# Block-sparse attention and SwiGLU on one core: later rows transposed by DMA, zero-tile matmuls ahead of the mask, a finer split of the first batch

## Chip, cores, metric

One Trainium2 chip, one core. The metric is device microseconds of one execution. A profiled execution also has a span (first to last instruction); the time is 1.7 to 2.3 us longer than the span in these runs.

## The reference, cut to what matters

```python
# B, H, S, D = 4, 8, 768, 64; blocks of 32, three random blocks per block row
scores = scale * q @ k.T ; scores = where(mask, scores, -1e9)
attn   = softmax(scores) @ v                       # per batch and head
x  = attn.transpose(0, 2, 1, 3).reshape(3072, 512)
xn = x / sqrt(mean(x * x) + 1e-6) * rms_g          # the "normed rows"
out = (silu(xn @ w_gate) * (xn @ w_val)) @ w_out   # 512 -> 1536 -> 512
```

## The kernel before

Work is cut into units: a batch, a first tile of 128 tokens and a number of tiles. A unit goes through attention for four pairs of heads (`qk`, `exp`, `av`, `xo`), normalisation (`sq`, `rsq`, `xq`), a transpose of its rows (`tr` on PE, `cp` on ACT or DVE), and the three weight products (`g`, `v`, `y`). A list scheduler in the kernel, with a guessed duration for each operation, fixes the order of instructions on every engine before anything runs.

```python
UNITS = [(0, 0, 1), (0, 1, 2), (0, 3, 3)]
UNITS += [(b, c, 3) for b in range(1, B) for c in (0, 3)]
...
nc.scalar.dma_start(out=gB, in_=moe_rms_g.unsqueeze(0).to_broadcast([P, DM]))   # the RMS gain
...
def turn(g):                # K and Q of batches 1 to 3: 24 tiles of 128 x 128
    nc.sync.dma_start_transpose(out=X[g % NSLOT]..., in_=aug[g % NAUG]...)
...
def tr(u):                  # rows of a unit: 4 transposes per tile on PE
    for t in range(nt):
        for c in range(NP):
            nc.tensor.transpose(out=t_[:, t, c, :], in_=xqs[u][:, t, c * P:(c + 1) * P], identity=ident)

def cp(u, eng):             # PSUM -> SBUF
    xns[u] = work.tile([P, NP, nt * P], BF16, name="xn", tag="xn", bufs=NXN)
    ...
def proj(u, f, w_, kind, pool):
    ...
    nc.tensor.matmul(out=p_[:, j, :], lhsT=w_[:, c, f_ * P:(f_ + 1) * P],
                     rhs=xns[u][:, c, :], start=(c == 0), stop=(c == NP - 1))
...
FILL0 = {"DVE": 0.57, "POOL": 0.84}     # casts of the first batch: on DVE or GpSimd
op(("zp",), {"POOL": 1.8}, [], (9,), lambda e, p: zero_pad(), at=18.0)
```

The softmax here doesn't subtract the row's maximum and nothing guards it: scores larger than these inputs give would overflow.

## Time and profile before

| | before |
|---|---|
| time, median of the first 4 runs | 322.04 us (321.62 to 323.87) |
| span of the profiled execution | 321.1 us (its time: 323.15) |
| PE busy | 304.5 us, 95% |
| first gate matmul | 32.59 us |

Engines: PE is TensorE, PEld its weight loads, DVE VectorE, ACT ScalarE, POOL GpSimd, SP SyncE, which issues DMAs. A busy PE may still run at half rate, so what follows compares the spacing of matmuls and not only busy shares. The prediction shows the lines.

### The profile page before, as it was taken

The page shows a single profiled execution, that of the slowest core. Times are in us where ns is not written, and L with a number is a line of the kernel's source. Part 1 is how long each engine was busy: PE and PEld are TensorE (multiplying, and loading weights), DVE is VectorE, ACT ScalarE, POOL GpSimd, SP SyncE. Part 2 cuts the span into 40 slices and gives each one's busy share as a digit, 9 for nine tenths or more (in the row PEclk, how much of TensorE's full clock was granted, in tenths as well). Part 3 has the DMA queues.
Part 4 walks back from the last instruction along what each step waited for, and adds up shares of the span by engine and source line. Part 5 has one row for each costly group of instructions (what it writes and reads, how often), then busy time and mean ns, then how long its engine had stood idle before and what let it go on. Part 6 is the DMA issues. An engine that isn't in the chain of part 4 may idle for free.

```text
span 321.1 us, 7025 instructions
## 1 busy us (share of the span) xinstructions
PE 304.5 (95%) x2903; PEld 200.0 (62%) x2934; DVE 193.9 (60%) x416; ACT 210.3 (65%) x312; POOL 24.9 (8%) x41
## 2 busy tenths in 40 slices
PE   2997999997999999999999999999999999999995
PEld 2886887774567666666666666666655656545542
DVE  5595676695358769546754844584567737717600
ACT  3588878895689777877777877877725323333221
POOL 4493000100001001000000100010010000000000
PEclk9999999999899999999999999999999999999999
DMA  7999997989986999600765000000000000020022
GB/s 223 369 194 204 245 270 156 258 283 185 279 276 144 216 243 263 234 3 33 100 132 98 35 36 0 35 2 33 3 33 35 0 35 34 0 97 3 0 100 98
DMA packets 59779, 40.03 MB, mean 125 GB/s; under 512 B 38628, under 2 KB 56548, under 8 KB 59748
## 3 DMA queue, kind: packets, MB, share of 16 engines
q1 hardware_dynamic: 53776, 34.61, 39.9%
q0 software_dynamic: 5792, 4.72, 9.5%
q8 instruction: 23, 0.38, 0.5%
q10 hardware_dynamic: 180, 0.26, 0.2%
q14 instruction: 8, 0.07, 0.1%
HBM read 28.57 MB, written 6.29 MB: 109 GB/s over the span
## 4 chain that ended last, share of the span: by engine, by line
PE 89%; DVE 4%; DMA 3%; ACT 2%; issue 1%; ACTq 0%; DVEq 0%
PE gp L331 19%; PE vp L331 19%; PE yp L363 18%; DMA X<-aug 2%; PE tp L212 2%; ACT pt L246 2%; PE tr L306 2%; DVE aug L182 1%; DMA samp_i<-in_sampled_blocks_dram 1%; DVE xq L296 1%; DVE sc L282 1%; DVE hp L354 0%; DVE xo L272 0%; PE o__3874 L260 0%; PE o__1140 L260 0%
## 5 line engine op out<-in xcount | busy, mean ns | idle before, releaser
L345 DVE SCALAR_TENSOR_TENSOR uu<-th,gp 128x384 bf16<-128x384 bf16 (+1 forms) x93 | 52.5, 566 | 60.8 <-ACT th L339 59.0
L331 PE MATMUL vp<-xn,wv 128*128 128x384 bf16 (+2 forms) x432 | 75.1, 309 | 0.3 <-DVE hp L354 0.3
L331 PE MATMUL gp<-xn,wg 128*128 128x384 bf16 (+2 forms) x432 | 75.1, 309 | 0.0
L339 ACT ACTIVATE th<-gp 128x384 bf16<-128x384 f32 (+1 forms) x93 | 46.6, 503 | 32.6 <-PE gp L331 30.5
L363 PE MATMUL yp<-wo,hp 128*128 128x512 bf16 x257 | 66.1, 381 | 1.8 <-issue 0.2
L354 DVE TENSOR_TENSOR hp<-uu,vp 128x384 bf16<-128x384 bf16 (+1 forms) x93 | 50.9, 563 | 11.4 <-PE vp L331 10.5
L331 PEld LDWEIGHTS <-wg 128*128 128x128 bf16 x432 | 40.3, 98 | 24.3 <-issue 0.8
L235 PEld LDWEIGHTS <-X 88*128 88x128 bf16 x432 | 38.9, 100 | 26.4 <-issue 4.3
L331 PEld LDWEIGHTS <-wv 128*128 128x128 bf16 x432 | 40.2, 97 | 24.4 <-issue 0.5
L363 PEld LDWEIGHTS <-hp 128*128 128x128 bf16 x288 | 28.2, 98 | 28.3 <-issue 0.5
L260 PEld LDWEIGHTS <-pt 128*128 128x128 bf16 x1152 | 41.6, 98 | 5.1 <-ACT pt L246 0.3
L372 ACT ACTIVATE yo<-yp 128x512 f32<-128x512 f32 x18 | 10.8, 599 | 24.2 <-PE yp L363 24.0
L289 POOL TENSOR_TENSOR rs<-ms,nhalf 128x3 f32<-128x3 f32 (+2 forms) x9 | 7.3, 806 | 207.3 <-DVE ms L282 207.3
L182 DVE CAST aug<-qkv 128x768 bf16<-128x768 f32 x30 | 17.7, 602 | 5.4 <-DMA X<-aug 3.2
L296 DVE SCALAR_TENSOR_TENSOR xq<-xo,rs,gB 128x512 bf16<-128x512 f32 x24 | 16.7, 746 | 1.0 <-POOL rs L289 0.7
L282 DVE CUSTOM_DVE_ANT_0 sc<-xo 128x512 bf16<-128x512 f32 x24 | 16.6, 690 | 0.7
L314 ACT COPY xn<-tr 128x1536 bf16<-128x1536 bf16 x7 | 10.1, 1437 | 7.9 <-PE tr L306 7.9
L212 PE MATMUL tp<-ident,aug 128*88 128x128 bf16 x96 | 9.0, 257 | 1.6 <-DVE aug L182 1.2
L212 PEld LDWEIGHTS <-aug 128*88 128x88 bf16 x96 | 8.2, 149 | 2.4 <-DVE aug L182 1.5
L182 DVE COPY X<-tp 88x768 bf16<-88x768 bf16 (+2 forms) x17 | 7.5, 473 | 3.6 <-PE tp L212 3.4
L182 DVE CAST vaug<-qkv 128x768 bf16<-128x768 f32 x14 | 7.7, 552 | 0.9 <-DMA qkv<-in_v_dram 0.9
L306 PE MATMUL tr<-ident,xq 128*128 128x128 bf16 x96 | 7.0, 219 | 0.1
(529 smaller groups left out, 359.0 us busy)
## 6 DMA issues: line engine op xcount, KB each, us to landing
qkv<-in_k_dram SPq DMA_DIRECT2D x16, 384.0 KB, 6.1
qkv<-in_q_dram SPq DMA_DIRECT2D x16, 384.0 KB, 6.1
qkv<-in_v_dram SPq DMA_DIRECT2D x16, 384.0 KB, 8.0
out_dram<-yo SPq DMA_DIRECT2D x24, 256.0 KB, 2.8
wg<-in_moe_w_gate_dram POOLq DMA_DIRECT2D x4, 384.0 KB, 8.8
wv<-in_moe_w_val_dram POOLq DMA_DIRECT2D x4, 384.0 KB, 9.9
wo<-in_moe_w_out_dram POOLq DMA_DIRECT2D x2, 768.0 KB, 18.3
gB<-in_moe_rms_g_dram ACTq DMA_DIRECT2D x1, 256.0 KB
```

Of the source, the lines that this page charges most:

```text
L182: nc.vector.tensor_copy(out=out, in_=in_)
L212: nc.tensor.transpose(out=t_[0:KQ, m, :], in_=aug[g % NAUG][:, i, e, c, 0:KQ], identity=ident)
L235: nc.tensor.matmul(out=s_[:, e, j * w:(j + 1) * w], lhsT=x[0:KQ, 0, e, jt * P:(jt + 1) * P], rhs=x[0:KQ, 1, e, c0 * P:c0 * P + w], start=T ...
L260: nc.tensor.matmul(out=o_[:, t, e, :], lhsT=pt[:, jt, e, t * P:(t + 1) * P], rhs=va[:, (2 * pr + e) * NC + jt, 0:D + 1], start=(jt == 0), ...
L282: nc.vector.tensor_tensor_reduce(out=sc, in0=x, in1=x, scale=1.0 / DM, scalar=1e-6, op0=ALU.mult, op1=ALU.add, accum_out=mss[u][:, t:t + 1])
L296: nc.vector.scalar_tensor_tensor(out=xqs[u][:, t, :], in0=xos[u][:, t].rearrange("p h d -> p (h d)"), scalar=mss[u][:, t:t + 1], in1=gB, o ...
L306: nc.tensor.transpose(out=t_[:, t, c, :], in_=xqs[u][:, t, c * P:(c + 1) * P], identity=ident)
L331: nc.tensor.matmul(out=p_[:, j, :], lhsT=w_[:, c, f_ * P:(f_ + 1) * P], rhs=xns[u][:, c, :], start=(c == 0), stop=(c == NP - 1))
L339: nc.scalar.activation(out=t_, in_=tiles["gp", u, f], func=AF.Tanh, scale=0.5)
L345: nc.vector.scalar_tensor_tensor(out=t_, in0=tiles.pop(("th", u, f)), scalar=1.0, in1=tiles.pop(("gp", u, f)), op0=ALU.add, op1=ALU.mult)
L354: nc.vector.tensor_tensor(out=hps[u][:, f * fg:(f + 1) * fg, :], in0=tiles.pop(("uu", u, f)), in1=tiles.pop(("vp", u, f)), op=ALU.mult)
L363: nc.tensor.matmul(out=y_, lhsT=hps[u][:, f, t * P:(t + 1) * P], rhs=wo[:, f, :], start=(f == 0), stop=(f == NF - 1))
```

## The change

The intent is to take 72 PE transposes off the bound, to have PE at full rate when real work comes, and to bring the first unit's rows to the weight products earlier. The diff, cut to its core:

```diff
-    UNITS = [(0, 0, 1), (0, 1, 2), (0, 3, 3)]
+    UNITS = [(0, 0, 1), (0, 1, 1), (0, 2, 2), (0, 4, 2)]
...
+    zt = const.tile([P, 512], BF16, name="zt")
+    nc.vector.memset(zt, 0.0)
+    zp = ps_a.tile([P, 512], FP32, name="zp", tag="vp")
+    for i in range(NWARM):                                  # NWARM = 9
+        nc.tensor.matmul(out=zp, lhsT=zt[:, 0:P], rhs=zt, start=True, stop=True)
...
-    nc.scalar.dma_start(out=gB, ...)                        # early, ACT's queue
+    def load_g():                                           # SP, after the first four pairs
+        nc.sync.dma_start(out=gB, in_=moe_rms_g.unsqueeze(0).to_broadcast([P, DM]))
...
-        xns[u] = work.tile([P, NP, nt * P], BF16, name="xn", tag="xn", bufs=NXN)
+        xns[u] = work.tile([P, nt, NP, P], BF16, name="xn", tag="xn", bufs=NXN)
+    def xt(u):
+        nc.sync.dma_start_transpose(
+            out=xns[u].rearrange("p t c w -> p (t c) w"),
+            in_=xqs[u].rearrange("p t f -> p (t f)"))
-                    ... rhs=xns[u][:, c, :],
+                    ... rhs=xns[u][:, :, c, :],
...
-    op(("zp",), ..., at=18.0)
+    op(("zp",), ..., at=26.0)                               # zero fill, later
-        op(("wi", i), {"POOL": 2.2 if i < NWC else 1.2},
+        op(("wi", i), {"POOL": 1.8 if i < NWC else 1.0},    # weight issue, guessed shorter
+        if u < NPET:                                        # NPET = 4: tr and cp as before
+        else:
+            op(("cp", u), {"DMA": 1.8}, ..., lambda e, p, u=u: xt(u), ...)
...                                                         # guessed time to landing of turn: 2 -> 4 us
+        end[...] = fin + (8.0 if ... else 4.0 if o["key"][0] == "turn" else LAT[e])
```

The diff also lets the scheduler count the buffers of `th` and `uu`, and changes two more of its guesses (`sq` from 0.62 to 0.75 us, the start of the DMA queue from 1.8 to 2.1). No run takes these, or the later zero fill, alone.

More of the change, by code (lines that the diff above doesn't have):

```diff
@@ L44 @@
     KQ = D + NB
-    NSLOT, NAUG, NRAW = 5, 2, 3
-    UNITS = [(0, 0, 1), (0, 1, 2), (0, 3, 3)]
+    NSLOT, NAUG, NRAW, NWARM = 5, 2, 3, 9
+    UNITS = [(0, 0, 1), (0, 1, 1), (0, 2, 2), (0, 4, 2)]
     UNITS += [(b, c, 3) for b in range(1, B) for c in (0, 3)]
@@ L148 @@
     nc.vector.memset(nhalf, -0.5)
-    nc.scalar.dma_start(out=gB, in_=moe_rms_g.unsqueeze(0).to_broadcast([P, DM]))
     wg = const.tile([P, DM // P, DFF], BF16, name="wg")
@@ L310, in cp @@
         nt = UNITS[u][2]
-        xns[u] = work.tile([P, NP, nt * P], BF16, name="xn", tag="xn", bufs=NXN)
-        o, i = xns[u].rearrange("p c (t w) -> p t c w", w=P), tiles.pop(("tr", u))[:, 0:nt]
+        xns[u] = work.tile([P, nt, NP, P], BF16, name="xn", tag="xn", bufs=NXN)
+        o, i = xns[u], tiles.pop(("tr", u))[:, 0:nt]
         if eng == "ACT":
@@ L316, in cp @@
             nc.vector.tensor_copy(out=o, in_=i)
+    def xt(u):
+        nt = UNITS[u][2]
+        xns[u] = work.tile([P, nt, NP, P], BF16, name="xn", tag="xn", bufs=NXN)
+        nc.sync.dma_start_transpose(
+            out=xns[u].rearrange("p t c w -> p (t c) w"),
+            in_=xqs[u].rearrange("p t f -> p (t f)"))
     def psum1(name, pool):
@@ L331, in proj @@
                 nc.tensor.matmul(
-                    out=p_[:, j, :], lhsT=w_[:, c, f_ * P:(f_ + 1) * P], rhs=xns[u][:, c, :],
+                    out=p_[:, j, :].rearrange("p (t w) -> p t w", w=P),
+                    lhsT=w_[:, c, f_ * P:(f_ + 1) * P], rhs=xns[u][:, :, c, :],
                     start=(c == 0), stop=(c == NP - 1))
@@ L376, in yo @@
         nc.sync.dma_start(out=dst[:, c0 + t, :], in_=o)
-    NPT, NXN, NHP = 3, 3, 2
+    NPT, NXN, NHP, NPET = 3, 3, 2, 4
     pools = {n: [0.0] * c for n, c in (
         ("s", 2), ("o", 1), ("gp", 1), ("vp", 1), ("acc", 1), ("pt", NPT), ("hp", NHP),
-        ("xo", 2), ("xq", 2), ("xn", NXN), ("raw", NRAW), ("va0", 1), ("va1", 1))}
+        ("xo", 2), ("xq", 2), ("xn", NXN), ("raw", NRAW), ("va0", 1), ("va1", 1), ("th", 2), ("uu", 3))}
     for i in range(NSLOT):
@@ L399 @@
     FILL0 = {"DVE": 0.57, "POOL": 0.84}
-    op(("zp",), {"POOL": 1.8}, [], (9,), lambda e, p: zero_pad(), at=18.0)
+    op(("zp",), {"POOL": 1.8}, [], (9,), lambda e, p: zero_pad(), at=26.0)
+    op(("lg",), {"DMA": 0.7}, [], (0,), lambda e, p: load_g())
     for g in range(B * NP):
@@ L444, in wi @@
             load_w(i) if i < NWC else load_wo(i - NWC)
-        op(("wi", i), {"POOL": 2.2 if i < NWC else 1.2},
+        op(("wi", i), {"POOL": 1.8 if i < NWC else 1.0},
            [("ld", 2, 0)] + ([("wi", i - 1)] if i else []), (2, i), wi)
         op(("w", i), {"DMA": 4.5}, [("wi", i)], (0,), None)
-    seq = [("ld", g, i) for g in range(NP) for i in range(3)]
+    seq = [("ld", g, i) for g in range(NP) for i in range(3)] + [("lg",)]
     for i in range(NWC + NOC):
@@ L482 @@
         for t in range(nt):
-            op(("sq", u, t), {"DVE": 0.62}, [("xo", u, NP - 1)], (1, u, t),
+            op(("sq", u, t), {"DVE": 0.75}, [("xo", u, NP - 1)], (1, u, t),
                lambda e, p, a=(u, t): sq(*a))
@@ L486 @@
         for t in range(nt):
-            op(("xq", u, t), {"DVE": 0.75}, [("rsq", u)], (1, u, t),
+            op(("xq", u, t), {"DVE": 0.75}, [("rsq", u), ("lg",)], (1, u, t),
                lambda e, p, a=(u, t): xq(*a), [("xq", u)],
                [("xo", u)] if t == nt - 1 else [])
-        op(("tr", u), {"PE": nt * NP * 0.056}, [("xq", u, t) for t in range(nt)], (0, u),
-           lambda e, p, u=u: tr(u), [("s", ("tr", u)), ("xn", u)], [("xq", u)])
-        op(("cp", u), {"ACT": 0.15 + nt * DM / 1200.0, "DVE": 0.17 + nt * DM / 1950.0}, [("tr", u)], (0, u),
-           lambda e, p, u=u: cp(u, e), [], [("s", ("tr", u))])
+        if u < NPET:
+            op(("tr", u), {"PE": nt * NP * 0.056}, [("xq", u, t) for t in range(nt)], (0, u),
+               lambda e, p, u=u: tr(u), [("s", ("tr", u)), ("xn", u)], [("xq", u)])
+            op(("cp", u), {"ACT": 0.15 + nt * DM / 1200.0, "DVE": 0.17 + nt * DM / 1950.0}, [("tr", u)], (0, u),
+               lambda e, p, u=u: cp(u, e), [], [("s", ("tr", u))])
+        else:
+            op(("cp", u), {"DMA": 1.8}, [("xq", u, t) for t in range(nt)], (-2, u),
+               lambda e, p, u=u: xt(u), [("xn", u)], [("xq", u)])
         wide = u >= NU - 4
@@ L502 @@
             op(("th", u, f), {"ACT": 0.12 + n_ / 1200.0}, [("g", u, f)], (2, u, f),
-               lambda e, p, a=(u, f): th(*a))
+               lambda e, p, a=(u, f): th(*a), [("th", (u, f))])
             op(("uu", u, f), {"DVE": 0.155 + n_ / 960.0}, [("th", u, f)], (2, u, f),
-               lambda e, p, a=(u, f): uu(*a), [], [(None, ("g", u, f))])
+               lambda e, p, a=(u, f): uu(*a), [("uu", (u, f))],
+               [(None, ("g", u, f)), ("th", (u, f))])
             op(("v", u, f), {"PE": fg * NP * mm(w)}, [("g", u, f)], (4, u, f, 0),
@@ L510 @@
             op(("hp", u, f), {"DVE": 0.155 + n_ / 960.0}, [("uu", u, f), ("v", u, f)], (3, u, f),
-               lambda e, p, a=(u, f): hp(*a), [], [(None, ("v", u, f))])
+               lambda e, p, a=(u, f): hp(*a), [],
+               [(None, ("v", u, f)), ("uu", (u, f))])
         for t in range(nt):
@@ L521 @@
                lambda e, p, a=(u, t): yo(*a, e), [], [(None, ("y", u, t))])
-    free = {"PE": 5.2, "ACT": 6.0, "DVE": 4.9, "POOL": 4.9, "DMA": 1.8}
+    free = {"PE": 5.2, "ACT": 6.0, "DVE": 4.9, "POOL": 4.9, "DMA": 2.1}
     left = {o["key"]: len(o["deps"]) for o in ops}
@@ L581 @@
         free[e] = fin
-        end[o["key"]] = fin + (8.0 if o["key"][0] == "ld" and o["key"][1] >= NP else LAT[e])
+        end[o["key"]] = fin + (
+            8.0 if o["key"][0] == "ld" and o["key"][1] >= NP else 4.0 if o["key"][0] == "turn"
+            else LAT[e])
         if o["key"][0] in ("qk", "tr"):
```

## The prediction

> **What bounds the kernel now.** I read the page first, then the chain of waits in order of time, the timeline of PE and of the DMA-issuing queue, the windows, and last the order of instructions of both built programs.
>
> ```profile
> PE 304.5 (95%) x2903; PEld 200.0 (62%) x2934; DVE 193.9 (60%) x416; ACT 210.3 (65%) x312; POOL 24.9 (8%) x41
> PE   2997999997999999999999999999999999999995
> PE 89%; DVE 4%; DMA 3%; ACT 2%; issue 1%; ACTq 0%; DVEq 0%
> ```
>
> PE is the bound: 95% busy, 89% of the chain that ended last. Only PE work taken away, or PE time lost, can move the end. Busy hides loss: instructions also count as busy when they run slowly. So I sum PE's program order at the spacing which the chain shows in the steady part: 56 ns for 128 columns, 109 for 256, 162.5 for 384, 216 for 512, 32 for 65. The kernel before has 297.8 us of such work, from 4.93 us (first matmul) to 317.12 (last). So 14.4 us are lost in between, and I place them stretch by stretch (elapsed less summed work):
>
> - 4.93 to 32.59 (first gate matmul): 27.66 for 18.31 of work, **9.35 lost**.
> - 32.59 to 75.16: 42.57 for 42.55, nothing lost.
> - 75.16 to 83.76: 8.60 for 4.55, **4.05 lost**.
> - 83.76 to 317.12: 233.36 for 232.42, 0.94 lost.
>
> The chain's early pieces (start us, us, what) show how the opening loses:
>
> ```profile
> 6.03 1.72 PE tp L212 x14
> 7.78 1.23 PE tp L212 x10
> 9.68 0.82 ACT pt L246
> 11.56 1.49 PE tp L212 x14
> 13.71 0.85 PE s__251 L235 x4
> 14.56 0.44 PE s__256 L235 x4
> 15.00 1.35 PE tp L212 x22
> 31.36 0.43 DVE xn L316
> 32.76 0.90 PE gp L331 x16
> ```
>
> Fourteen transposes cost 1.49 us (106 ns each), and four 256-column matmuls 0.85 us, then 0.44 us for the same four: PE runs at half rate until about 14.4 (the granted clock reads 1.00 there; the spacing tells, not that column). The rest of the opening is waits for exponentials, evictions and loads. The first gate matmul waits for the first unit's normed rows (xn at 31.36).
>
> The second loss, in PE's timeline (start, us, ..., idle before):
>
> ```profile
> 75.16 0.81 PE L331 MATMUL gp<-xn,wg 128*128 128x384 bf16 x4
> 77.72 0.50 PE L235 MATMUL s__1464<-X 88*128 88x384 bf16 x2 [1.75 <-DMA X<-aug]
> 81.59 0.84 PE L235 MATMUL s__1494<-X 88*128 88x384 bf16 x2
> 83.76 0.49 PE L235 MATMUL s__1509<-X 88*128 88x384 bf16 x2
> ```
>
> A transposed K/Q tile of the second batch came late, PE idled 1.75 us, then ran at half rate (0.84 for what otherwise takes 0.49):
>
> ```profile
> 77.72:84.00 6.28, 5.76 (x23) 2.82 (x25) 3.05 (x7) 3.48 (x5) 0.00 (x0) 0.73 1.13 251
> ```
>
> Granted clock 0.73 over 6.28 us is 3.4 us at half rate (6.28 x 0.27 x 2), 1.7 us lost. The chain gives this tile 7.40 us from 70.27; the queue shows how long its issue holds the queue:
>
> ```profile
> 70.27 8.23 SPq L194 DMA_TRANSPOSE X<-aug  x2
> 78.56 0.57 SPq L70 DMA_DIRECT2D qkv<-in_k_dram  x1
> ```
>
> **What the Trainium skill says.** "TensorE: Matmul & The Clock Gate", section "What's actually happening": the array starts at half rate and is released after a busy window of about 3.4 us, which is free-running. The trace agrees in kind (half rate until 14.4, then a step; 3.4 us of it after the stall). Section "Wait — 56ns, not 53.3ns?" of that page: 106.7 ns between 128-column matmuls when cold, 55.6 when warm; here 106 and 56. "DMA: Bandwidth & Descriptors", section "DMA Transpose (X-bar)": two-byte types only, into SBUF, from SP or ACT; the rows are bf16, and the 12 X transposes already go this way from SP. "SBUF — State Buffer", section "Who interferes with whom": casts on DVE can be blocked by GpSimd on a shared port pair. The trace agrees: two casts at 18.59 took 2.17 us beside a GpSimd cast and its weight issues, where one alone takes 0.55. It matters as more early casts now go to GpSimd.
>
> **The change part by part.**
>
> *Row transposes by DMA.* The last six of ten units lose 12 PE transposes each: 72 x 56 ns = 4.0 us of PE, all on the bound, and one ACT copy each (6 x 1.44 = 8.6 us, which buys nothing while PE binds). Added: six DMA transposes on SP, half the size of an X one. An X takes 3.6 to 4.4 us of issue and 5.8 (once 7.4) to landing; I estimate 2.2 and 4. Of these six, the program order leaves the first the least room: the unit's rows are ready about 8 us before its first gate matmul, but an X transpose of 4.4 us precedes it in SP's order, so some 1 to 2.5 us remain. The later five have one to two units of other PE work ahead of them, over 10 us.
>
> *Smaller first units.* Same number of transposes, value matmuls and output matmuls; a few more instructions at the floor of 2.5 ns. Summed order without the zero-tile matmuls: 294.17 us, 3.66 less than before, so the split costs about 0.4 us. Before the first gate matmul PE has 17.73 us of work (18.31 before), after it 276.44 (279.52).
>
> *Zero-tile matmuls.* Nine of 512 columns: 9 x 427 ns cold = 3.8 us, in time in which PE waits (before, it waited 4.9 us for the mask). From about 1.4 us they end near 5.3, perhaps 0.3 us into the mask's time, but the transposes wait for a cast until 6.03 anyway. They should leave PE warm at or soon after 6. The zero fill of some 0.3 us on DVE fits the 0.94 us in which DVE waits for the block list.
>
> *The first gate matmul.* Warm, the 24 first transposes need 1.34 instead of 2.95 us; evictions hide some of it, so the first exponential starts at about 8.5 instead of 9.68. From there ACT sets the pace: 16 exponentials of 768 columns (0.70 us apart) and 4 of 1024 (0.92) stand before the row copy, 14.9 us, plus 0.5 for the copy. ACT's waits between 9.7 and 31 sum to about 5.1 us, of which the longest, 2.0, is for cold transposes; I keep 3.1. Sum 27.0; add 0.7 for semaphores and queueing at the end and 0.8 for the third and fourth pair's casts on GpSimd (0.82 there, 0.55 on DVE, behind two weight issues). The first gate matmul at **28.5** instead of 32.59. Weights just allow it: the second chunk, issued at 16.5 to 17.4 and landing 8.8 to 9.9 later, was there by 25 to 27; it now stands behind three GpSimd casts, some 2 us, of which part is hidden while the first chunk moves.
>
> *The stall at 75.16.* The scheduler now allows more time to landing for an X transpose. By the summed order its tile is used at 67.2 - 19.7 = 47.5 us after the first gate matmul, so at 76, and its casts stand at about 67: with 5.8 to 7.4 us it lands at 73 to 74.5. I expect the 4.05 us to go mostly, and keep 2.2 us of losses in all for the rest (0.94 as before, 1.3 for small stalls on either kind of transpose).
>
> Sum of the span: 28.5 + 276.4 + 2.2 + 4.0 (last output from 317.12 to 321.1) = 311.1, that is 10.0 below 321.1. Off the median of 322.11: **312.1 us**.
>
> **The rivals.** *The opening is bound elsewhere.* If loads of the four pairs or the weights pace it, warming PE only lengthens waits. For: DMA is at 9 in most early slices, PE already has gaps there, and the third weight chunk, landing at 28.8 to 30.5, would be wanted at 32.6, with less room than before. Against: the longest ACT wait was for cold PE work. It would make the first gate matmul 31, the time 314.6. *A transpose is the new wait.* SP issues in order, and an X of 4.4 us, loads and outputs can stand before a row transpose. For: 8.23 us for two, and 1 to 2.5 us of room for the first. Against: five of six have much more. One such wait costs about 2 + 1.7 us of half rate: 315 to 316; two: 319. *The old stall stays:* with all else as I say, 316. *The new row layout slows the gate and value matmuls*, whose moving operand is now in pieces of 128 columns: 10 ns on each of the 768 with 256 or 384 columns would be 7.7 us. Nothing in the trace speaks for it; before, the row was one piece.
>
> **Range and chances.** The first gate matmul is uncertain by 1.5 us either way, the losses after it run from 1 to 5, and the first three rivals are partly exclusive. That gives 309 to 316.5 for 8 in 10. 2% faster is below 315.7: it takes two of the rivals together, or one large, to miss it. Faster 0.83, same 0.15, slower 0.02.
>
> **What would show it.** Right: first transposes (24) in 1.4 us; first exponential near 8.5; first gate matmul near 28.5; 24 row transposes on PE instead of 96, six on SP; no PE wait above 1 us after 30, clock 1.00 all through; gate matmuls of 384 columns still 162 ns apart. Wrong: the zero-tile matmuls end and PE still runs at 106 ns (the window missed); PE waits for xn or X by DMA with the clock below 1 after it; the first gate matmul past 30 with ACT or PE waiting for loads or weights.

## The result, and the profile after

313.7 us median (313.06 to 314.48, 4 runs) against 322.04. The ratio is 0.9732, 95% interval 0.9688 to 0.9775. A ratio here is the mean time of one kernel's fast runs over the mean of the other's of the same rounds, so it is not quite the ratio of the medians. The profiled execution has a span of 311.3 us.

The page of the kernel after: PE's row, its busy tenths, and the chain by engine.

```profile
PE 300.7 (97%) x3015; PEld 201.8 (65%) x3015; DVE 188.0 (60%) x411; ACT 204.1 (66%) x306; POOL 26.3 (8%) x44
PE   6899999998999999999999999999999999999994
PE 90%; DMA 5%; ACT 2%; DVE 1%; SPq 0%; issue 0%; POOL 0%; ACTq 0%; DVEq 0%
```

PE is still the bound, with less work and less lost time. The opening in the chain of waits (start us, us, what):

```profile
10.51 1.04 PE tp L220 x14
12.27 0.44 PE s__271 L243 x4
13.99 0.67 PE tp L220 x12
28.73 0.89 PE gp L346 x16
```

Four 256-column matmuls take 0.44 us at 12.27, where before they took 0.85 as late as 13.71. The first gate matmul starts at 28.56 by PE's timeline. In the two places where PE waited longest after that, PE's timeline shows:

```profile
77.36 1.03 PE L346 MATMUL gp<-xn,wg 128*128 128x256 bf16 x8 [0.80 <-DVE uu L361]
146.46 0.48 PE L243 MATMUL s__2762<-X 88*128 88x384 bf16 x2 [0.63 <-ACT pt L254]
```

The stall of 1.75 us on a transposed tile is gone, and no half rate follows: the granted clock from 75 to 84 is 1.00; before, it was 0.73 from 77.72 to 84. DVE's timeline tells what the 0.80 us are:

```profile
75.22 1.03 DVE L190 CAST aug<-qkv 128x768 bf16<-128x768 f32 x2 [1.86 <-DMA X<-aug]
76.16 0.55 DVE L190 CAST vaug<-qkv 128x768 bf16<-128x768 f32 x1
76.63 0.68 DVE L361 SCALAR_TENSOR_TENSOR uu<-th,gp 128x512 bf16<-128x512 bf16 x1
```

A K/Q transpose now delays PE by another way. DVE takes its instructions in order; a cast waits until the DMA has read its buffer, and `uu`, which would free PE's PSUM bank, stands behind three casts.

The row transposes, in SP's timeline (start, us held by the issue), then in the list of DMA issues (count, median us to landing):

```profile
98.21 4.53 SPq L202 DMA_TRANSPOSE X<-aug  x1
103.26 1.45 SPq L329 DMA_TRANSPOSE xn<-xq  x1
```

```profile
X<-aug SPq DMA_TRANSPOSE x12, 6.1
xn<-xq SPq DMA_TRANSPOSE x6, 4.0
```

The first one lands 4.0 us after 103.26, and its unit's first gate matmul comes at 108.69 by PE's timeline, so about 1.4 us of room remain.

The new row layout does not slow the matmuls. Groups by form (busy us, mean ns | idle before), before:

```profile
L331 PE MATMUL gp<-xn,wg 128*128 128x384 bf16 x336 | 65.7, 327 | 0.0
```

and after:

```profile
L346 PE MATMUL gp<-xn,wg 128*128 128x384 bf16 x288 | 55.5, 326 | 0.0
```

Laid out as in the prediction (summed PE order at the steady spacing, elapsed time less that sum):

| us, profiled executions | before | after |
|---|---|---|
| PE work, zero-tile matmuls left out | 297.8 | 294.2 |
| lost before the first gate matmul, from the span's start | 14.28 | 10.83 |
| lost after it, to PE's last instruction | 5.0 | 2.2 |
| last output | 4.0 | 4.1 |
| span | 321.1 | 311.3 |

For "lost before": 32.59 less 18.31 of work, and 28.56 less 17.73.

### The profile page after: what moved, and what is told of

Same layout as the page of the kernel before. It is cut to its first block, busy times and chain, and to the rows that moved or that the text cites. A ratio compares the mean times of both kernels' runs of the same rounds, so it can differ in the third digit from the quotient of the medians.

```text
span 311.3 us, 7229 instructions
## 1 busy us (share of the span) xinstructions
PE 300.7 (97%) x3015; PEld 201.8 (65%) x3015; DVE 188.0 (60%) x411; ACT 204.1 (66%) x306; POOL 26.3 (8%) x44
## 4 chain that ended last, share of the span: by engine, by line
PE 90%; DMA 5%; ACT 2%; DVE 1%; SPq 0%; issue 0%; POOL 0%; ACTq 0%; DVEq 0%
PE gp L346 20%; PE yp L379 20%; PE vp L346 20%; DMA X<-aug 2%; DMA qkv<-in_k_dram 2%; ACT pt L254 2%; PE tp L220 1%; PE tr L314 0%; SPq L70 0%; PE o__3524 L268 0%; PE o__2246 L268 0%; PE o__2882 L268 0%; PE o__1425 L268 0%; PE o__3944 L268 0%; PE o__3095 L268 0%; PE o__2679 L268 0%
## 5 line engine op out<-in xcount | busy, mean ns | idle before, releaser
L379 PE MATMUL yp<-wo,hp 128*128 128x512 bf16 x288 | 69.7, 379 | 0.0
L355 ACT ACTIVATE th<-gp 128x384 bf16<-128x384 f32 (+1 forms) x90 | 46.3, 514 | 33.5 <-PE gp L346 31.5
L346 PEld LDWEIGHTS <-wg 128*128 128x128 bf16 x480 | 43.2, 98 | 22.6 <-issue 1.0
L370 DVE TENSOR_TENSOR hp<-uu,vp 128x384 bf16<-128x384 bf16 (+1 forms) x90 | 50.3, 577 | 12.0 <-PE vp L346 11.2
L346 PEld LDWEIGHTS <-wv 128*128 128x128 bf16 x480 | 43.1, 97 | 21.2
L243 PEld LDWEIGHTS <-X 88*128 88x128 bf16 x480 | 40.8, 97 | 20.1 <-issue 2.2
L388 ACT ACTIVATE yo<-yp 128x512 f32<-128x512 f32 x23 | 13.8, 598 | 29.9 <-PE yp L379 29.6
L190 DVE CAST aug<-qkv 128x768 bf16<-128x768 f32 x28 | 15.3, 560 | 4.8 <-DMA X<-aug 3.6
L220 PE MATMUL tp<-ident,aug 128*88 128x128 bf16 x96 | 7.2, 220 | 1.8 <-DVE aug L190 0.8
L220 PEld LDWEIGHTS <-aug 128*88 128x88 bf16 x96 | 6.0, 120 | 2.4 <-POOL aug L188 0.9
L88 PE MATMUL zp<-zt 128*128 128x512 bf16 x9 | 3.5, 564 | 1.3 <-DVE zt L85 1.3
L188 POOL CAST aug<-qkv 128x768 bf16<-128x768 f32 x4 | 3.3, 834 | 5.0 <-DMA qkv<-in_k_dram 5.0
```

What stands on the lines that cost most here:

```text
L190: nc.vector.tensor_copy(out=out, in_=in_)
L220: nc.tensor.transpose(out=t_[0:KQ, m, :], in_=aug[g % NAUG][:, i, e, c, 0:KQ], identity=ident)
L243: nc.tensor.matmul(out=s_[:, e, j * w:(j + 1) * w], lhsT=x[0:KQ, 0, e, jt * P:(jt + 1) * P], rhs=x[0:KQ, 1, e, c0 * P:c0 * P + w], start=T ...
L346: nc.tensor.matmul(out=p_[:, j, :].rearrange("p (t w) -> p t w", w=P), lhsT=w_[:, c, f_ * P:(f_ + 1) * P], rhs=xns[u][:, :, c, :], start=( ...
L355: nc.scalar.activation(out=t_, in_=tiles["gp", u, f], func=AF.Tanh, scale=0.5)
L370: nc.vector.tensor_tensor(out=hps[u][:, f * fg:(f + 1) * fg, :], in0=tiles.pop(("uu", u, f)), in1=tiles.pop(("vp", u, f)), op=ALU.mult)
```

## The experiments

All were correct. Ratios are to the kernel before, from the runs of the same call. The kernel after has 0.9732 there, and 0.9737 in its repeat. An effect in us below is a difference of ratios times 322.5.

| run | ratio | 95% | first gate matmul (profiled) |
|---|---|---|---|
| after without the zero-tile matmuls | 0.9798 | 0.9753 to 0.9843 | 28.8 |
| after with all rows on PE | 0.9873 | 0.9842 to 0.9905 | 29.2 |
| after with the old units | 0.9844 | 0.9810 to 0.9878 | 29.4 |
| after with the old time to landing | 0.9730 | 0.9699 to 0.9762 | 27.6 |
| before with the new time to landing | 0.9985 | 0.9966 to 1.0004 | 31.5 |
| before with the zero-tile matmuls | 0.9969 | 0.9946 to 0.9993 | 31.4 |
| before with the rows by DMA | 0.9903 | 0.9878 to 0.9928 | 32.1 |
| before with the new units | 0.9935 | 0.9904 to 0.9966 | 31.1 |
| after, repeated | 0.9737 | 0.9688 to 0.9786 | 30.8 |
| after with the gap filled | 0.9739 | 0.9690 to 0.9788 | 28.3 |
| after with three cast buffers | 0.9719 | 0.9672 to 0.9766 | 31.95 (slow state) |
| after with the gain loaded early | 0.9726 | 0.9687 to 0.9765 | 29.6 |

**1. No zero-tile matmuls.** The order of everything else is the same.

```diff
-    for i in range(NWARM):
+    for i in range(0):
```

> The changed kernel without the nine zero-tile matmuls; every other instruction stands in the same order. Theory A (PE's half rate paced the opening): PE runs at half rate until about 14, the transposes of the first four pairs at 106 ns again; since PE is dense from 10.5 on in the changed kernel, that costs about 2 us: first gate matmul near 30.5, span near 313.5. Rival (loads and ACT pace the opening): first gate matmul within 0.5 us of 28.6, span within 0.5 us of 311.3.

The time rose by 2.1 us, but the profiled execution does not show it where it was expected: its first gate matmul stands at 28.8, not at 30.5. PE came to full rate at 9.8 us by the trace's clock record (before: 14.4, after: 4.1; the record begins with this release, and the views print 1.00 ahead of it). A release at 14.4 was seen only once: of the five profiles without zero-tile matmuls four have it at 9.7 to 10.4, and that of before at 14.4. Of the eight profiles with nine of them, four have it at 4.1 to 4.9 and four at 9.8 to 10.2.

The 0.2 us between 28.8 and 28.56 do not measure what an early release is worth, because the loads also landed at different times. The cast of the second pair's K on GpSimd waits for its load. In POOL's timeline it starts in the kernel after at

```profile
9.63 0.82 POOL L188 CAST aug<-qkv 128x768 bf16<-128x768 f32 x1 [4.73 <-DMA qkv<-in_k_dram]
```

and in this run at

```profile
8.43 0.89 POOL L188 CAST aug<-qkv 128x768 bf16<-128x768 f32 x1 [3.54 <-DMA qkv<-in_k_dram]
```

Up to the first gate matmul, and zero-tile matmuls aside, the kernel after and the first, second and fourth run have the same order on every engine, so their profiles give like pairs. With casts at 8.43 and 8.53, release at 9.8 gives 28.78 and release at 4.1 gives 27.63. With casts at 9.41 and 9.63, release at 10.0 gives 29.15 and release at 4.1 gives 28.56. So an early release was worth 0.6 to 1.2 us at the first gate matmul and, given an early release, an early landing 0.9 us.

The other five executions of this run have spans from 312.7 to 317.3, and for those no trace exists. The 2.1 us have intervals of 1.5 and 1.4 us, on this run and on the kernel after; together with the sixth run (1.0 us, interval 0.8) they show that the zero-tile matmuls help on average. In which executions the gain lies is not shown.

This execution also shows the narrow room of the row transposes, in PE's timeline:

```profile
108.93 0.81 PE L346 MATMUL gp<-xn,wg 128*128 128x384 bf16 x4 [0.82 <-DMA xn<-xq]
```

**2. All rows on PE.** `NPET = 4` becomes 99.

> The changed kernel with all row transposes on PE, nothing else undone. Theory A (each PE transpose stands on the bound): 72 transposes by 56 ns = 4.0 us longer, span near 315.3, first gate matmul unchanged near 28.6. Rival 1 (the DMA transposes cost waits that eat part of it): under 3 us longer. Rival 2 (PE has slack where they stood): under 1 us longer.

4.5 us longer, with intervals of 1.0 us on each side for this run and 1.4 for the kernel after: in agreement with 4.0, and clearly against rival 2; rival 1 is unlikely. Although the nine zero-tile matmuls ran in it, this execution reached full rate only at 10.0: they do not secure an early release.

**3. The old units** (`NPET = 3`, so that the same six units go by DMA).

```diff
-    UNITS = [(0, 0, 1), (0, 1, 1), (0, 2, 2), (0, 4, 2)]
+    UNITS = [(0, 0, 1), (0, 1, 2), (0, 3, 3)]
```

> The changed kernel with the first batch in units of 128, 256 and 384 tokens again (six later units by DMA as before). Theory A (warm PE gives most of the earlier first gate matmul, smaller units a part of it): first gate matmul 0.5 to 1.5 us later, near 29.6, PE work 0.4 us less, span 0.2 to 1.2 us longer, if no other wait comes of the new order. Rival (the smaller units give most of it): first gate matmul 2 us later or more, span 2 us longer or more.

3.6 us longer: more than theory A allows. The first gate matmul is 0.9 us later, as it says; most of the rest comes after it: laid out as in the table above, 5.8 us are lost there against 2.2. PE's waits of this run count 2.3 us of gate matmuls waiting for `uu` on DVE, by the way just described, at 75.66 for 1.24 us of it. In the first profile after it is 0.8, but 1.8 in the repeat of the unaltered kernel (eighth run), so these waits locate at most a part of it; the rest stays open.

**4. The old time to landing.** The `4.0 ... "turn"` term goes.

> The changed kernel with the scheduler's time to landing for the K/Q transposes put back from 4 to 2 us. Theory A (that constant took away the stall on the transposed tile): the stall at about 75 returns, 1 to 2 us of PE idle and then up to 3.4 us of half rate, span 3 to 4 us longer. Rival (the stall went because the smaller units gave PE other work at that place): span within 1 us of 311.3 and clock 1.0 throughout.

No change. The stall does return, in PE's timeline:

```profile
74.15 0.50 PE L243 MATMUL s__1599<-X 88*128 88x384 bf16 x2 [1.35 <-DMA X<-aug]
```

but 1.35 us long and in this execution without half rate after it, and the wait of 0.80 us for `uu` is gone. (Its first gate matmul, 1 us earlier, is not the constant's work: up to there every engine has the same order as in the kernel after, and the loads landed 1.1 us earlier.) So the constant trades one wait for the other; it is not what made the kernel faster.

**5 to 7. One part alone in the kernel before.** The time to landing:

> The kernel before with only the scheduler's time to landing for the K/Q transposes raised from 2 to 4 us. The fourth experiment showed that without it the changed kernel loses hardly anything. Theory A (either the constant or the new units moves the tile's use late enough, so one alone is sufficient): the idle time of 1.75 us and the 3.4 us of half rate go, 2.5 to 4 us shorter than before. Rival (the constant does nothing anywhere): within 1 us of before.

The zero-tile matmuls:

> The kernel before with only the nine zero-tile matmuls in front; the order of all else is untouched. Theory A (half rate paced the opening): PE at full rate from some moment between 4 and 10 us instead of 14.4, depending on where the clock's window falls in that execution, and 1.5 to 2.5 us shorter than before on average. Rival (loads and ACT pace it): within 0.7 us of before. The stall near 75 stays in both.

The rows by DMA (the new `xn` layout, `xt`, `NPET = 3`):

> The kernel before with only the six later units' rows transposed by DMA (and the row layout that goes with it). Theory A: 4.0 us less PE work, 4 us shorter than before, if the stall near 75 stays as it is; the clock's half-rate opening stays. Rival (a DMA transpose turns into a wait where the opening is later and SP's order another): under 2 us shorter, with a PE wait on xn or on X by DMA and half rate after it.

They gave 0.5 (not told apart from nothing: the interval is 0.6), 1.0 and 3.1 us. The constant does take the stall away (the clock stays at 1.0), yet its new order waits 1.60 us for `hp` at 108, and theory A's 2.5 us were not there. The zero-tile matmuls gave somewhat less than expected; in the profiled execution the release came at 10.0. The rows gave 3.1 rather than 4.0, with the old stall in its place (1.80 us at 77.31).

The many executions of before in these calls show what half rate costs. By the mean granted clock of an execution, 24 of 91 kept full rate (clock at least 0.9985): median span 319.4. 58 had a clock near 0.995, one stretch of 3.4 us at half rate: 320.9. Nine had less: 322.4. With the stall taken away, in the time-to-landing run, 15 of 22 stayed at 0.9985 or above, and 19 at 0.997 or above. So half rate in the same program is a matter of the execution, and one stretch costs 1.5 us; that it lies at the stall is seen in the profiled ones alone. The profile before, at 0.995 and 321.1, was not the best that this kernel does.

**8. The kernel after again, and 9. the gap filled.** Three more zero-tile matmuls of 256 columns after the mask's, in the 0.8 us before the first cast:

```diff
+    for i in range(3):
+        nc.tensor.matmul(out=zp[:, 0:256], lhsT=zt[:, 0:P], rhs=zt[:, 0:256], start=True, stop=True)
```

> The changed kernel again, unaltered, as the measure for the others of this call. Both theories: ratio to before near 0.973, span between 311 and 313. If the moment at which PE comes to full rate is a matter of where its window falls, it need not be at 4.1 us as in the first profile, but may lie anywhere up to about 10.

> The changed kernel with three more zero-tile matmuls of 256 columns after the mask's matmuls, in the 0.8 us in which PE waits for the first cast. Theory A (a window that holds that gap does not count as busy, so the release comes either at 4.0 to 5.4 us or only at 8.8 to 10.8): the release now lies between 4.0 and 7.4. It is worth little on time, 0.2 to 0.5 us on average. Rival (the gap does not matter to the release): release as late as 8 to 10 in some executions, no gain.

Filling the gap changed nothing in time. Its release came at 4.6, which the unfilled kernel can also have, so whether the gap matters stays open. The repeat is worth more: its profiled execution has a span of 314.7 and a first gate matmul at 30.8, with the same program. DVE's timeline, in the kernel after as first profiled:

```profile
13.83 0.55 DVE L190 CAST aug<-qkv 128x768 bf16<-128x768 f32 x1
```

and in its repeat:

```profile
14.15 2.82 DVE L190 CAST aug<-qkv 128x768 bf16<-128x768 f32 x1
```

The same cast took 2.82 us instead of 0.55. POOL's timeline of the repeat:

```profile
14.19 0.84 POOL L188 CAST vaug<-qkv 128x768 bf16<-128x768 f32 x1
14.95 1.60 POOL L188 CAST aug<-qkv 128x768 bf16<-128x768 f32 x2
```

and its PE:

```profile
17.03 0.31 PE L220 MATMUL tp<-ident,aug 128*88 128x128 bf16 x2 [1.71 <-DVE aug L190]
```

GpSimd started three casts in a row just after DVE's start, and DVE's ended only after the last of them, at 16.97. In the first profile the DVE cast was done at 14.38 and the row of three began at 15.45. The change had put two more early casts on GpSimd; here, where the loads landed so that they met DVE's, PE lost 1.7 us.

**10. The new units alone in the kernel before.**

> The kernel before with only the new units of the first batch. Undoing them in the changed kernel cost 3.6 us. Theory B (the small units, not the full rate of PE, bring the first gate matmul forward, because both first units are through attention before ACT turns to the wide exponentials): first gate matmul 2 to 3 us earlier than 31.5, span 2 to 4 us shorter than before. Theory A of the prediction (warm PE brings most of it): first gate matmul under 1.5 us earlier, span within 1.5 us of before.

In its fast runs 2.1 us shorter than before, inside theory B. The first gate matmul at 31.1 seems to speak against it, but this order puts 19.81 us of PE work ahead of it, not 18.31: 11.3 us lost, where the two single-part runs with release near 10 (the time to landing, the zero-tile matmuls) lose 13.1 to 13.2. So the units cut 1.8 us of opening loss here; "earlier first gate matmul" was the wrong yardstick. (Undone in the kernel after, in the third run, the opening loss rose only from 10.8 to 11.1, with loads that landed 0.7 us earlier.) The old stall is still there, 1.40 us at 75.18, so the units alone do not take it away. Ten of its 21 executions were slow by the rule (over 1.5% above the fastest), with clocks of 0.988 to 0.994. None of them was profiled, and their cause stays open. The gain thus holds for the fast executions only: the median of all 21, 323.47, is above that of before, 322.51.

**11. Three buffers in front of the K/Q transposes** (`NAUG = 3`, `NSLOT = 4`, the third buffer's mask copied by ACT and GpSimd).

> The changed kernel with three instead of two buffers in front of the K/Q transposes, and four instead of five behind them, which frees the memory. Theory (the wait of 0.8 us for DVE near 77 is a cast that stands in DVE's order and waits until a transpose has read its buffer): that wait goes, and up to 1 us comes off, unless the fourth slot is missed later on. Rival (DVE is late there for other reasons, or the slot is missed): no gain, or a wait for X by DMA later on and a longer time.

The wait near 77 is gone, as the theory says; others for `uu` come later (0.35 us at 116.77, 0.30 at 121.14, and one of 1.04 at 155.70). The time is not told apart from the kernel after. Its profiled execution fell in the slow state and serves only to show a mechanism, the held-up cast in full length. DVE, then PE:

```profile
13.25 3.30 DVE L192 CAST aug<-qkv 128x768 bf16<-128x768 f32 x1
```

```profile
16.61 0.31 PE L222 MATMUL tp<-ident,aug 128*88 128x128 bf16 x2 [2.19 <-DVE aug L192]
```

The windows after it (engines' busy us, then clock, DMA share, GB/s):

```profile
18.40:22.00 3.60, 3.60 (x46) 3.40 (x42) 2.12 (x7) 1.78 (x2) 2.98 (x4) 0.54 1.32 202
```

PE idled 2.19 us and then had a granted clock of 0.54: the late cast cost the wait and a stretch at half rate, although PE had been at full rate since 4.7.

**12. The gain loaded early again.**

```diff
+    nc.scalar.dma_start(out=gB, in_=moe_rms_g.unsqueeze(0).to_broadcast([P, DM]))
-    op(("lg",), {"DMA": 0.7}, [], (0,), lambda e, p: load_g())
+    op(("lg",), {"DMA": 0.7}, [], (0,), None)
```

> The changed kernel with the load of the RMS gain (256 KB, broadcast over 128 partitions) back on ACT's queue at the start, as before; the order on all engines but SP and ACT's queue is untouched. With new units and no warm-up the first gate matmul stood at 28.8, with the new units alone in the kernel before at 31.1, so something else in the change brings some 2.3 us. Theory C (it is this load, which no longer stands among the loads of the first pairs): the third pair's K is cast about 1.1 us later and the first gate matmul comes 1 to 2.3 us later, the time is 1 to 2 us longer. Rival D (it is the scheduler's other constants: later zero fill, more casts on GpSimd): first gate matmul within 0.5 us of 28.6 in an execution whose DVE casts are not held up, time within 0.7 us of the changed kernel.

The third pair's K is cast at 13.75, against 11.2 to 12.7 in the profiles that load the gain late, and the first gate matmul comes at 29.64 instead of 28.78 (first run) and 29.15 (second run) at a like release (9.8 to 10.0). That is theory C in kind, but 0.5 to 0.9 us and not 1 to 2.3, in single profiles, and the time is the same. The expectation overlooked where most of its 2.3 us come from: the order of the tenth run puts 2.1 us more PE work ahead of the first gate matmul (19.81 against 17.73). Single shares of the scheduler's other constants were not measured.

No version was shown to be faster than the kernel after.

## Why the prediction was right, point by point

**PE is the bound, and its work falls by 3.66 us.** Right. Without the DMA transposes the time was 4.5 us longer; alone in the kernel before they gave 3.1; the step said 4.0. An estimated issue of 2.2 us per row transpose was 1.45, the landing of 4 was 4.0, and the "1 to 2.5 us of room" were about 1.4. In one execution the room failed by 0.82 us.

**The first gate matmul at 28.5.** It was at 28.56, but the step that led there was partly wrong. It gave the whole 4 us to a warm PE and to ACT's waits. The first exponential did come at 8.57 (8.5 predicted), but the prediction counted from one profile with a release at 14.4, where profiles without zero-tile matmuls mostly had it near 10. The runs show that the zero-tile matmuls are worth 1.0 to 2.1 us on average, that a release near 4 instead of near 10 gains 0.6 to 1.2 us at the first gate matmul in profiles whose loads land alike, and that the finer units cut 1.8 us of opening loss in the kernel before, where the prediction gave them 0.6 us less of PE work and nothing more. It did not speak of the gain's load at all, which is worth 0.5 to 0.9 us there in single profiles and nothing shown in the time. Hitting 28.5 was luck in part: with the same order up to that point four profiles have 27.63, 28.56, 29.15 and 30.81.

**"They should leave PE warm at or soon after 6."** In the first profile 4.1, but 9.8 to 10.2 in four of the eight profiles with the same nine matmuls. The mechanism holds, the certainty did not.

**Casts on GpSimd, 0.8 us.** The named mechanism (DVE blocked by GpSimd) was right, the size was that of an undisturbed cast. In two profiles in which they met, the DVE cast took 2.8 to 3.3 us and PE lost 1.7 to 2.2; in a third (the first run) the GpSimd cast was the one held up, 1.28 us instead of 0.84.

**The stall mostly gone, 2.2 us of losses left.** Measured 2.2. The reason given, the scheduler's longer time to landing, holds for the stall itself (it returns without the constant, and is gone with the constant alone), but it is not what counts in the time: without it the time is the same.

**From span to time.** The span was predicted at 311.1 and was 311.3; the time was predicted at 312.1 and was 313.7. The missing 1.6 us lie between the profiles and the medians: the working took 10.0 us off a profiled span of 321.1 and subtracted that from the median time, although the profiled execution, at 323.15, was itself 1.0 us slower than that median. And the first profile after, at 313.06, was the fastest of its four, 0.6 us below their median.

The single parts do not add up: alone they give 0.5 + 1.0 + 3.1 + 2.1 = 6.7 us of about 8.6. Undone one by one, rows, units and zero tile sum to 10.3. They may share waits, and parts that no run took alone may bring the rest; the runs do not tell these apart.

## What to carry to other kernels

Sum the bound engine's program order at its steady spacing, and place what is lost: that gave a span within 0.2 us, with luck in the opening, and without it busy time hides half rate. Anchor the forecast on the median execution, or profile more than one, since the same program lost 1.5 us more in some, and its loads landed 1.0 us apart in two profiles; compare openings only between profiles with like loads and a like release. Before moving fp32 casts to GpSimd, look whether several stand in a row where DVE has one on the critical path.

## What the Trainium skill lacked or had wrong

- "TensorE: Matmul & The Clock Gate", section "What's actually happening", puts the cold state after at least one idle window of about 3.4 us. Here an idle time of 1.75 us, and one of 2.19, were followed by 3.4 us at half rate; of the kernel before, whose profile shows such a stall, 67 of 91 executions had a clock below 0.9985. Waits of 1.35 to 1.71 us in five other profiles were not followed by it.
- The same section does not say how busy a window has to be to release the clock. With PE at work from 1.26 us the release came at 4.1 in one execution (0.6 us idle in the 3.4 before it), and at 10.0 to 10.2 in three others, where PE was idle for 0.5 to 0.8 us just before the first transposes (at 6.08 to 6.44).
- "SBUF — State Buffer", section "Who interferes with whom", says that the second to issue is blocked for the other's instruction. Here a DVE cast stayed blocked through three GpSimd casts back to back, 2.82 and 3.30 us instead of 0.55, although the trace has its start before theirs (14.15 against 14.19, 13.25 against 13.76). In the first run the GpSimd cast was recorded first (14.09 against 14.15), and it was the one that was held up: 1.28 us instead of 0.84. The recorded starts, which are rough on GpSimd, do not foretell here who waits.
- "DMA: Bandwidth & Descriptors", section "DMA Transpose (X-bar)", has no time for which a transpose between SBUF places holds its issuing queue (the page has a sequencer count for one only in its part on a trn3 build). In the kernel after: 1.42 to 1.46 us in most cases (5.01 once) for 12 tiles of 128 by 128, landing after 4.0; 3.7 to 5.4 us for 24 tiles, landing after 6.1.
